# Transposing half of an activation by DMA, moving V's turn to a task of its own, opening a gate one step earlier, and putting PV before projections at the end in a statically scheduled attention kernel

## The chip, the cores and the metric

The kernel runs on one core of a Trainium2 chip. The metric is the device time of one execution in microseconds (us). The profiled execution of each kernel shows a span (first to last instruction) which is 1.7 to 3.5 us shorter than the device time of the same execution. All executions compared here are fast: none is more than 1.5% above the fastest of its kernel. TensorE does matrix products, VectorE and GpSimd elementwise work, ScalarE the exponentials; SyncE (SP) issues all DMAs.

## The reference

Two attention blocks over 2048 tokens, width 1024, 32 heads of 32, concatenated. A is plain softmax attention. B works on four segments of 512 tokens: causal softmax attention inside the segment, plus a read of a memory that earlier segments have written.

```
a:  q,k,v = x @ wqkv ;  o = softmax(q k^T / sqrt(32)) v ;  out = o @ wo
b:  for s in range(4):                      # segments of 512
        a_dot = softmax(q_s k_s^T / sqrt(32) + causal mask) v_s
        a_mem = (phi(q_s) @ M) / (phi(q_s) @ z + 1e-6)
        o_s   = sigmoid(beta) * a_mem + (1 - sigmoid(beta)) * a_dot
        M += phi(k_s)^T v_s ;  z += sum(phi(k_s))
    out = o @ wo
```

## The kernel before

The kernel is written by a scheduler. At build time it plays the program with a table of estimated costs, keeps a list of tasks (generators that yield what they wait for), and appends instructions to each engine's program in the order in which they would start. On the chip that order is fixed; only semaphore waits adapt. So a changed cost number or a changed condition moves the order of everything after it.

Scores of A come in 64 units (group g of four heads, 256 queries c), those of B in 32. A unit of A is 16 exponentials of 128x1024. `pick` takes the next unit from A or B. TensorE writes scores, ScalarE takes the exponential, TensorE multiplies by V ("PV") and sums the rows, VectorE normalises (`finish`), and projections (`out_proj`) follow.

```
def loads(self):                                  # A's x: 16 tiles of 128 rows
    for k in range(16):
        tile_in(k)                                # plain DMA
        if k == 1: self.load_WA(0, 0)             # weights of the keys
        if k == 3: self.load_WA(1, 0)             # queries
        if k == 5: self.load_WA(2, 0)             # V

def turn_A(self):                                 # each tile turned by 8 TensorE transposes
    for k in range(16):
        ...
        yield ("pe", self.ready(keys))
        def f(e): ... e.transpose(self.psb[:, bank, ...], src[...], self.ident[:, :])
        ...                                       # then one copy out by VectorE (two by ScalarE)

def a_prep(self, g):                              # keys, queries, V of one group
    for c in range(4):                            # chunks of 512 tokens
        yield ("ev", ("xA", c))                   # (g == 0)
        yield from proj(0, c)                     # keys
        self.events.add(("kA", g, c))
        if early:                                 # first group only
            if c == 0:
                ...
                yield from proj(1, 0)             # queries of chunk 0
                self.events.add(("sA", g, 0))
            yield from proj_V(c)                  # V in line, turned by a small DMA transpose

def pick(self):
    ...
    if b and b.kn >= 8 and ("amem", b.kn) not in self.events:
        b = None                                  # B barred until its memory read is done
    if a and b:
        it = b if b.kn < a.kn * SLOPE + LEAD else a

# b_prep(n), from segment 1 on: the memory read
    ...  den = Zb^T PH + 1e-6                     # one matmul, one VectorE op
    for q in range(4): reciprocal(den[:, cs])     # four VectorE ops
    ...  amem = (Mb^T PH) * gA * den
    self.events.add(("amem", n))

# schedule(): what TensorE does next when no scores are due
    full = len(self.ring_busy) > HIGH
    first = self.run if STICK and self.run else ("pv" if full else "side")
```

`self.run` is what TensorE did last, so the last line keeps it at projections ("side") or at PV. "Chunk" below is 512 keys of the first unit of A: four exponentials.

## Time and profile before

The median of the first three runs is 1203.21 us (1202.05 to 1205.38). The span of the profiled run is 1198.7 us. First the page's busy times by engine (PE is TensorE's matmul, PEld its weight load, DVE VectorE, ACT ScalarE).

```profile
span 1198.7 us, 37080 instructions
PE 1042.5 (87%) x16699; PEld 481.9 (40%) x16927; DVE 803.4 (67%) x1363; ACT 1125.4 (94%) x1256; POOL 116.5 (10%) x192
```

ScalarE is the limit. Its 1216 exponentials cannot be removed, so a schedule can win only its idle time. The view of busy time by stretch, for four stretches that I chose (the last begins when the last exponential ends):

```profile
core 0: us, PE busy (x) PEld busy (x) DVE busy (x) ACT busy (x) POOL busy (x), PEclk, DMA share, GB/s
0.00:16.00 16.00, 12.48 (x94) 6.92 (x96) 8.14 (x14) 3.55 (x5) 4.06 (x16) 1.00 0.94 293
16.00:54.00 38.00, 34.06 (x389) 15.48 (x394) 14.83 (x24) 23.97 (x29) 0.00 (x0) 1.00 0.25 56
54.00:1168.30 1114.30, 976.22 (x16114) 450.73 (x16323) 769.49 (x1307) 1097.89 (x1224) 112.39 (x176) 0.97 0.23 52
1168.30:1198.70 30.40, 19.70 (x117) 8.74 (x117) 10.99 (x20) 0.00 (x0) 0.00 (x0) 0.87 0.15 55
```

In each line the count of instructions is in brackets; PEclk is the share of its full clock that TensorE was granted, DMA share the mean busy share of the 16 DMA engines. Length less ScalarE's busy time is its idle: 12.4, 14.0, 16.4 and 30.4 us. I call these stretches first loads, start, middle and end. All idle numbers below are worked out like this.

The start, in the timeline of ScalarE (start, duration, operation, count, and in brackets the idle time before and what ended it):

```profile
15.99 3.77 ACT L532 ACTIVATE PT<-ps 128x1024 bf16<-128x1024 f32 x4 [6.09 <-PE ps L506]
23.68 0.77 ACT L467 ACTIVATE gcol<-ps 32x8 f32<-32x8 f32 x4 [3.92 <-PE ps L462]
26.70 3.83 ACT L532 ACTIVATE PT<-ps 128x1024 bf16<-128x1024 f32 x4 [2.25 <-PE ps L506]
33.49 3.77 ACT L532 ACTIVATE PT<-ps 128x1024 bf16<-128x1024 f32 x4 [2.97 <-PE ps L506]
39.80 9.27 ACT L532 ACTIVATE PT<-ps 128x1024 bf16<-128x1024 f32 x10 [2.53 <-PE ps L506]
51.34 18.44 ACT L532 ACTIVATE PT<-ps 128x1024 bf16<-128x1024 f32 x20 [2.27 <-PE ps L506]
```

The first four exponentials of each chunk start at 16.0, 26.7, 33.5 and 39.8, with waits for scores between.

The end, in the timeline of all engines (L674 with xA,OTA is A's output projection, L591 to L612 the normalisation of the last unit):

```profile
1163.39 4.84 ACT L532 ACTIVATE PT<-ps 128x1024 bf16<-128x1024 f32 x5
1166.10 12.03 PE L674 MATMUL ps<-xA,OTA 128*128 128x512 bf16 x54 [0.16 <-issue]
1179.05 0.28 PE L581 MATMUL ps<-PT,ones 128*32 128x256 bf16 x4
1179.39 0.69 DVE L591 COPY OL<-ps 128x512 f32<-128x512 f32 x1 [0.53 <-PE ps L581]
1182.56 0.42 DVE L612 TENSOR_TENSOR OTA<-OL,SQ 128x256 bf16<-128x256 f32 x1
1183.04 1.14 PE L674 MATMUL ps<-xA,OTA 128*128 128x512 bf16 x4 [3.70 <-DVE OTA L612]
```

TensorE still owes projection matmuls of earlier units when the exponentials end: a block of 54 starts at 1166.1, 2 us before that. The last PV comes after them, and then TensorE waits 3.7 us for the normalisation.

The view by tile, from 1000 us on, shows the scores of B (first line: tile KQB) and B's own output projection (second line: tile WoB). Duration min/median/max in ns, then first and last start:

```profile
L506 PE MATMUL ps<-KQB x72: 214/309/416, 1000.8 to 1061.2; 32*128 32x256 bf16 x48, 32*128 32x128 bf16 x24
L674 PE MATMUL ps<-WoB,OTB x58: 379/379/390, 1075.6 to 1102.8; 128*128 128x512 bf16 x58
```

### The profile page before, as it was taken

What the parts mean: (1) busy time and instruction counts of PE and PEld (TensorE: products, weight loads), DVE (VectorE), ACT (ScalarE), POOL (GpSimd) and SP (SyncE); (2) the same over time, 40 slices, a digit from 0 to 9 for tenths busy, and PEclk for the clock granted to TensorE, in tenths of its full rate; (3) what the DMA queues carried; (4) which work ended last, traced back from release to release, by engine and by line L of the source; (5) the groups of instructions that cost most, each with busy time, mean ns of one, the idle gap of its engine ahead of it and who ended that gap; (6) DMA issues with size and microseconds to landing.
All of it is one profiled execution on the core that took longest, in us unless ns stands there. A gap on an engine that the chain in (4) does not pass through costs nothing.

```text
span 1198.7 us, 37080 instructions
## 1 busy us (share of the span) xinstructions
PE 1042.5 (87%) x16699; PEld 481.9 (40%) x16927; DVE 803.4 (67%) x1363; ACT 1125.4 (94%) x1256; POOL 116.5 (10%) x192
## 2 busy tenths in 40 slices
PE   8998889999888888888988897978989887789996
PEld 4343444444344333334444443434444343334442
DVE  5248567576786687866777768677777668774443
ACT  3799999999999999999999999999999999999990
POOL 1001001010101020200111102010110102010000
PEclk9999999999999979899999998989999898989998
DMA  5461132243111122141212121211221110401101
GB/s 172 100 162 38 32 86 59 60 89 76 42 37 41 39 48 54 31 82 32 68 38 45 46 50 37 60 24 37 49 66 41 32 42 15 102 20 37 37 37 56
DMA packets 198344, 66.45 MB, mean 55 GB/s; under 512 B 189986, under 2 KB 189986, under 8 KB 198178
## 3 DMA queue, kind: packets, MB, share of 16 engines
q1 hardware_dynamic: 198178, 63.99, 23.1%
q8 instruction: 135, 2.21, 0.8%
q14 instruction: 31, 0.25, 0.1%
HBM read 39.85 MB, written 8.39 MB: 40 GB/s over the span
## 4 chain that ended last, share of the span: by engine, by line
ACT 47%; PE 40%; DVE 10%; issue 3%; DMA 1%; SPq 0%; DVEq 0%
ACT PT L532 46%; PE ps L674 21%; PE ps L581 9%; PE ps L506 8%; DVE SQ L604 2%; DVE OL L591 2%; DVE den L870 1%; ACT E L844 1%; DVE OL L608 1%; DVE amem L877 1%; DMA OTA<-in_A_x_dram 1%; DVE OTA L612 0%; DVE den L864 0%; DVE outsb L919 0%; DMA out_dram<-outsb 0%
## 5 line engine op out<-in xcount | busy, mean ns | idle before, releaser
L532 ACT ACTIVATE PT<-ps 128x1024 bf16<-128x1024 f32 (+1 forms) x1216 | 1102.4, 1039 | 32.4 <-PE ps L506 30.1
L581 PE MATMUL ps<-PT,ones 128*32 128x256 bf16 (+1 forms) x4864 | 295.6, 275 | 0.0
L581 PE MATMUL ps<-PT,VA 128*32 128x256 bf16 x4096 | 251.8, 277 | 20.9 <-ACT PT L532 15.0
L506 PE MATMUL ps<-QA,KA 32*128 32x256 bf16 x4096 | 213.2, 277 | 39.6 <-ACT PT L532 31.3
L604 DVE RECIPROCAL SQ<-OL 128x128 f32<-128x128 f32 x256 | 242.8, 948 | 4.9
L674 PE MATMUL ps<-xB,WB 128*128 128x512 bf16 x684 | 179.2, 383 | 21.2 <-issue 11.6
L674 PE MATMUL ps<-xA,WA 128*128 128x512 bf16 x695 | 181.6, 387 | 16.5 <-issue 8.7
L506 PEld LDWEIGHTS ps<-QA,KA 32*128 32x128 bf16 x4096 | 62.7, 92 | 224.8 <-ACT PT L532 201.0
L581 PEld LDWEIGHTS ps<-PT,VA 128*32 128x32 bf16 x4096 | 108.2, 95 | 111.3 <-issue 65.3
L552 POOL TENSOR_SCALAR_AFFINE_SELECT PT<-PT 128x512 bf16<-128x512 bf16 x128 | 85.9, 672 | 666.3 <-ACT PT L532 661.2
L581 PEld LDWEIGHTS ps<-PT,ones 128*32 128x32 bf16 x4864 | 131.6, 98 | 2.5
L591 DVE COPY OL<-ps 128x512 f32<-128x512 f32 x128 | 85.6, 669 | 30.3 <-PE ps L581 29.4
L674 PEld LDWEIGHTS ps<-xA,WA 128*128 128x128 bf16 x768 | 63.2, 99 | 93.9 <-issue 27.9
L674 PEld LDWEIGHTS ps<-xB,WB 128*128 128x128 bf16 x768 | 61.8, 98 | 95.2 <-issue 45.3
L919 DVE CAST outsb<-ps 128x512 bf16<-128x512 f32 x64 | 43.5, 680 | 76.2 <-PE ps L674 71.4
L870 DVE RECIPROCAL den<-den 128x128 f32<-128x128 f32 x96 | 91.2, 950 | 2.3
L684 DVE CAST KQB<-ps 128x512 bf16<-128x512 f32 x64 | 43.7, 683 | 57.8 <-PE ps L674 57.4
L674 PE MATMUL ps<-xA,OTA 128*128 128x512 bf16 x236 | 59.5, 391 | 8.5 <-DVE OTA L612 3.7
L674 PE MATMUL ps<-WoB,OTB 128*128 128x512 bf16 x232 | 59.7, 380 | 6.6 <-issue 2.9
L581 PE MATMUL ps<-PT,VB 128*32 128x256 bf16 (+1 forms) x768 | 50.8, 282 | 15.3 <-DVE OL L591 12.0
L608 DVE SCALAR_TENSOR_TENSOR OL<-OL,SQ 128x256 f32<-128x256 f32 x128 | 58.2, 455 | 2.7
L684 DVE CAST VT<-ps 128x512 bf16<-128x512 f32 x32 | 22.0, 687 | 47.7 <-PE ps L674 44.3
(64 smaller groups left out, 490.9 us busy)
## 6 DMA issues: line engine op xcount, KB each, us to landing
WB<-in_B_wk_dram SPq DMA_DIRECT2D x32, 256.0 KB, 3.0
WB<-in_B_wq_dram SPq DMA_DIRECT2D x32, 256.0 KB, 2.9
WB<-in_B_wv_dram SPq DMA_DIRECT2D x32, 256.0 KB, 3.2
out_dram<-outsb SPq DMA_DIRECT2D x32, 256.0 KB, 2.0
WA<-in_A_wqkv_dram SPq DMA_DIRECT2D x24, 256.0 KB, 3.8
OTA<-in_A_x_dram SPq DMA_DIRECT2D x16, 256.0 KB, 5.6
WoB<-in_B_wo_dram SPq DMA_DIRECT2D x1, 2048.0 KB, 10.2
xA<-in_A_wo_dram SPq DMA_DIRECT2D x1, 2048.0 KB, 10.3
```

Source lines behind the costliest of these rows:

```text
L506: ins = e.matmul(o, l, r, start=True, stop=True)
L532: op = R.op("ACT", lambda e: e.activation(self.PT[:, s0:s0 + n, 0:width], self.ps[:, banks[0]:banks[0] + n, 0:width], ACTF.Exp, bias=cb, s ...
L552: mo = R.op("POOL", lambda e, ap=ap, pat=pat: e.affine_select(ap, ap, pattern=pat, compare_op=ALU.is_ge, fill=0.0, base=0, channel_multipl ...
L581: ins = e.matmul(o, l, r, start=start, stop=end, skip_group_check=True)
L591: R.op("DVE", lambda e: e.tensor_copy(self.OL[x][:, :], self.ps[:, OLB, :]), r=[("ps", OLB)], w=[("OL", x)], cost=0.66)
L604: R.op("DVE", lambda e, cs=cs: e.reciprocal(rec[:, cs], L[:, cs]), r=[ko], w=[k], cost=0.93)
L608: R.op("DVE", lambda e: e.scalar_tensor_tensor(L, L, 1.0, rec, ALU.mult, ALU.add, accum_out=self.rng[:, u.seq:u.seq + 1]), r=[k, ko], w=[k ...
L674: ins = e.matmul(o, l, rh, start=a, stop=z)
L684: op = self.R.op("DVE", lambda e: e.tensor_copy(dst, self.ps[:, bank, :]), r=[("ps", bank)], w=[dkey], cost=0.66)
L844: ex = R.op("ACT", lambda e: e.activation(self.E[:, k0:k1, :], KQ[:, k0:k1, :], ACTF.Exp), r=[("KQB", b, k) for k in range(k0, k1)], w=["E ...
L870: R.op("DVE", lambda e, cs=cs: e.reciprocal(self.den[:, cs], self.den[:, cs]), r=["den"], w=["den"], cost=0.9)
L919: op = R.op("DVE", lambda e, ns=ns, bank=bank, ob=ob: e.tensor_copy(self.outsb[ob][:, ns], self.ps[:, bank, :]), r=[("ps", bank)], w=[("ou ...
```

## The change

Its intent: the first keys need not wait for 16 tiles to be turned on TensorE, V of the first group need not sit between two key projections, and B's scores need not wait for the memory read. Five parts can be told apart: (1) chunks 2 and 3 of A's x are loaded by one DMA transpose each, only eight tiles are turned on TensorE; (2) the first V runs in a task of its own, one chunk behind the keys, turned by TensorE; two PSUM banks (buffers into which TensorE writes) lent to these tasks go back earlier; (3) B's scores are gated on the sum in the denominator ("den") and the finish of the unit waits for the memory read instead; (4) when the banks of the scores have been given up at the end, PV goes before projections; (5) the planning numbers for the load of B's x.

```
+TURNS = 2
+GATE = "den"
@@ load_xB                                                    # (5)
-                   ..., issue=5.0, mb=1.0)
+                   ..., issue=1.0, mb=2.0)
@@ loads, turn_A                                              # (1)
-        for k in range(16):
+        for k in range(4 * TURNS):
             tile_in(k)
...
-            if k == 5:
+            if k == 4 * TURNS - 1:
                 self.load_WA(2, 0)
+        for c in range(TURNS, 4):
+            R.dma(lambda e, c=c: e.dma_start(self.xA[:, :, 512*c:512*c+512],
+                  self.A_x[0][512*c:512*c+512, :], transpose=True), ..., issue=1.0, mb=2.0)
+            self.events.add(("xA", c))
@@ a_prep                                                     # (2)
+            if early:
+                ...                            # 4 TensorE transposes, one VectorE copy
+            else:
+                self.turn_V(vt[:, :], key, dst, ("VA", b, c))
+        def values():
+            yield ("ev", ("WA", 2, g))
+            for c in range(4):
+                yield ("ev", ("kA", g, min(c + 1, 3)))
+                yield from proj_V(c)
+            self.load_WA(2, g + 1)
...
-                    yield ("ev", ("WA", 2, g))
-                yield from proj_V(c)
+                    self.spawn(values(), (-1, 1.5), "valuesA0")
@@ schedule                                                   # (2)
-            if self.lent and ("vA", 0, 3) in ev:
+            if self.lent and ("vA", 0, 2) in ev:
...
-                if not self.bank_busy & set(self.lent) and nslot == 0:
+                if not self.bank_busy & set(self.lent):
@@ finish, b_prep, pick                                       # (3)
             else:
+                yield ("ev", ("amem", u.kn))
...
+            self.events.add(("den", n))        # right after the sum, before the reciprocals
...
-        if b and b.kn >= 8 and ("amem", b.kn) not in self.events:
+        if b and b.kn >= 8 and (GATE, b.kn) not in self.events:
@@ schedule                                                   # (4)
-            full = len(self.ring_busy) > HIGH
-            first = self.run if STICK and self.run else ("pv" if full else "side")
+            full = len(self.ring_busy) > HIGH or not self.slots
+            first = self.run if STICK and self.run and self.slots else ("pv" if full else "side")
```

More of the change, by code (lines that the diff above doesn't have):

```diff
@@ L368, in load_xB @@
         self.R.dma(lambda e: e.dma_start(self.xB[b][:, :, :], src, transpose=True),
-                   w=[("xB", b, i) for i in range(NI)], issue=5.0, mb=1.0)
+                   w=[("xB", b, i) for i in range(NI)], issue=1.0, mb=2.0)
         self.events.add(("xB", s))
@@ L387, in loads @@
                 self.load_WA(1, 0)
-            if k == 5:
+            if k == 4 * TURNS - 1:
                 self.load_WA(2, 0)
+        for c in range(TURNS, 4):
+            R.dma(lambda e, c=c: e.dma_start(self.xA[:, :, 512 * c:512 * c + 512], self.A_x[0][512 * c:512 * c + 512, :], transpose=True),
+                  w=[("xA", i, c) for i in range(NI)], issue=1.0, mb=2.0)
+            self.events.add(("xA", c))
         R.dma(lambda e: e.dma_start(self.beta[0:1, :], self.B_beta.rearrange("(a n) -> a n", a=1)), w=["beta"], issue=0.5, mb=0.01)
@@ L405, in turn_A @@
         R = self.R
-        for k in range(16):
+        for k in range(4 * TURNS):
             src, keys = self.stage(k)
@@ L728, in a_prep @@
         k_ = 0
+        early = g == 0 and not self.shifted
         def pace():
@@ L745, in proj_V, with f @@
             yield from self.proj_T(self.WA[2], ("WA", 2), lambda i: self.xA[:, i, cs], lambda i: ("xA", i, c), vt[:, :], key)
-            self.turn_V(vt[:, :], key, self.VA[b][:, 4 * c:4 * c + 4, :], ("VA", b, c))
-            self.events.add(("vA", g, c))
+            dst = self.VA[b][:, 4 * c:4 * c + 4, :]
+            if early:
+                bank = yield ("bank",)
+                yield ("pe", self.ready([key]))
+                def f(e, bank=bank):
+                    for t in range(4):
+                        ins = e.transpose(self.psb[:, bank, P * t:P * t + P], vt[:, P * t:P * t + P], self.ident[:, :])
+                    return ins
+                R.op("PE", f, r=[key, "ident"], w=[("ps", bank)], cost=0.3)
+                op = R.op("DVE", lambda e, bank=bank: e.tensor_copy(dst, self.psb[:, bank, 0:512].rearrange("p (t n) -> p t n", t=4)),
+                          r=[("ps", bank)], w=[("VA", b, c)], cost=0.36)
+                self.bank_release(bank, op)
+            else:
+                self.turn_V(vt[:, :], key, dst, ("VA", b, c))
+            self.events.add(("vA", g, c))
+        def values():
[4 more added lines that the diff above has]
+            self.load_WA(2, g + 1)
         def total(k):
@@ L753, in total @@
                  r=[("cbt", b, 0), ("cbt", b, 1 + k)], w=[("cbA", b, k)], cost=0.1)
-        early = g == 0 and not self.shifted
         yield ("ev", ("WA", 0, g))
@@ L774, in a_prep @@
         yield from self.a_norm(g, 0, range(4), cb[:, 4:5], ("cbt", b, 0))
+        if early:
+            yield ("ev", ("vA", g, 3))
         for c in range(1 if early else 0, 4):
@@ L789, in a_prep @@
             self.load_WA(1, g + 1)
-            self.load_WA(2, g + 1)
+            if not early:
+                self.load_WA(2, g + 1)
         else:
```

## The prediction

> **What bounds it now.** ScalarE: busy 1125.4 of 1198.7 us (94%), 1102.4 of it the 1216 exponentials of 1.04 us. The change removes none, so it can only win from 73 us of idle. The view of busy time by stretch places them: 0-16 us, 12.4 idle; 16-54 us, 14.0 idle; 54-1168 us, 16.4 idle in 1114; 1168-1199 us, 30.4 idle. TensorE is busy 87%.
>
> **16-54 us.** ScalarE's timeline shows bursts of four exponentials (3.8 us), one per chunk of keys, starting at 16.0, 26.7, 33.5 and 39.8, with waits for scores between, and 2.3 us more before 51.3. TensorE fills them: transposing the other 11-12 tiles of x until 21.8, then keys and V of a chunk one after the other (1.7-1.9 us each, plus 1.4 us until the scores start).
>
> **Removed and added.** Half of 128 TensorE transposes goes (8 tiles, each about 0.6 us on TensorE and a 0.69 us copy on VectorE: 5 us of each). Added: two DMA transposes of 1 MB. B's x has the same shape: 4.4-5.7 us to issue, 7.7-8.4 to land (about 130 GB/s; the Trainium skill, "DMA: Bandwidth & Descriptors", Latency and other measured facts, gives 261 GB/s for one kernel; this trace is slower and I use the trace). Issued after eight tile loads, near 7.5 and 12.5 us, they should land near 16-17 and 21-23. Four DMA turns of V (2.4 us to landing) become 16 TensorE transposes and four copies, about 0.3 + 0.4-0.7 us each.
>
> **On the critical path.** Keys of chunk 1 need no longer wait for 12 tiles and V: their exponentials can follow the first burst (about 20 instead of 26.7). Chunk 2 follows near 24-25. Chunk 3 is ordered late by the static schedule: near 30-32, not 39.8. I expect 8-10 us saved here, and 1-2 of the wait before 51.3, as the lent banks return earlier. The first key projection waits in TensorE's order for the fifth tile, landed at 9.75; with one weight load later, up to 0.5 us.
>
> **Tail.** After the last exponential (1168.2) TensorE runs 54 projection matmuls, 12 us, before the last PV (1178.1-1179.3), then idles 3.7 us for the normalisation. The change prefers PV once the score banks are given up. That normalisation then hides under the projections: about 3.5 us saved.
>
> **B's gate.** Scores of B may start when the denominator is summed, about four reciprocals (3.8 us) and a matmul earlier. While B is barred A's scores run instead, so ScalarE is fed: all its waits for scores after 200 us are 12.1 us, in 19 pieces, many where the granted clock is 0.86-0.93. I expect 0-3 us. Reordering may shift the middle by +-4 us.
>
> **Sum.** -9 -1.5 -0.3 -3.5 -1 = about -15: 1188 us. Two per cent would need 24 us.
>
> **Signs.** If right, the second, third and fourth bursts start near 20, 25 and 31; ScalarE's idle in 16-54 falls from 14 to 3-5; 54-1168 keeps about 1102 us busy with 13-17 idle; the last PV comes directly after the last exponential and the 3.7 us wait is gone.
>
> **What would make it wrong.** The two transposes block SP's queue for some 10 us or land past 25 us (chunk 3 then near 36 or later, gain 4 less); they slow the last tile loads; V, now a task with higher priority, pushes the keys back; finishing B units, which now waits for the memory read, holds back PV and fills the ring; TensorE is throttled longer.

## The result, and the profile after

The changed kernel takes 1187.83 us (median of 4, 1186.62 to 1190.14); the kernel before, over the runs taken by then, 1202.63 us (median of 4). The ratio is 0.988, with a 95% interval of 0.985 to 0.991. A ratio here is the mean time of one kernel's fast runs over that of the other's of the same rounds, so not quite the ratio of the medians.

The total lies on the predicted 1188. The parts do not. The page and the view by stretch, after:

```profile
span 1184.9 us, 36949 instructions
PE 1028.6 (87%) x16650; PEld 480.5 (41%) x16880; DVE 796.3 (67%) x1359; ACT 1124.7 (95%) x1256; POOL 116.3 (10%) x192
```

```profile
0.00:16.00 16.00, 12.71 (x100) 7.24 (x101) 8.75 (x15) 3.54 (x4) 4.08 (x16) 1.00 0.98 253
16.00:54.00 38.00, 34.80 (x467) 15.48 (x470) 12.62 (x23) 31.34 (x37) 0.00 (x0) 1.00 0.58 107
54.00:1164.90 1110.90, 970.64 (x16040) 453.43 (x16254) 767.06 (x1306) 1089.80 (x1216) 112.18 (x176) 0.97 0.22 51
1164.90:1184.90 20.00, 10.45 (x61) 4.34 (x59) 7.92 (x15) 0.04 (x1) 0.00 (x0) 0.88 0.12 44
```

| idle of ScalarE, us | first loads | start | middle | end |
|---|---|---|---|---|
| before | 12.4 | 14.0 | 16.4 | 30.4 |
| predicted change | -0.3 | -9 to -11 | about -1 | -3.5 |
| after | 12.5 | 6.7 | 21.1 | 20.0 |
| measured change | 0 | -7.3 | +4.7 | -10.4 |

The start gained less than predicted, the end three times as much, and the middle gave 4.7 us of these 17.7 back. The timeline of ScalarE at the start, after:

```profile
16.23 7.49 ACT L538 ACTIVATE PT<-ps 128x1024 bf16<-128x1024 f32 x8 [6.53 <-PE ps L512]
25.48 1.94 ACT L538 ACTIVATE PT<-ps 128x1024 bf16<-128x1024 f32 x2 [1.76 <-PE ps L512]
28.42 1.94 ACT L538 ACTIVATE PT<-ps 128x1024 bf16<-128x1024 f32 x2 [1.00 <-PE ps L512]
32.22 2.85 ACT L538 ACTIVATE PT<-ps 128x1024 bf16<-128x1024 f32 x3 [1.86 <-PE ps L512]
34.95 0.76 ACT L473 ACTIVATE gcol<-ps 32x8 f32<-32x8 f32 x4
40.39 18.52 ACT L538 ACTIVATE PT<-ps 128x1024 bf16<-128x1024 f32 x20 [1.65 <-PE ps L512]
```

The first two chunks are now one run of eight exponentials; chunks 3 and 4 start at 25.5 and 32.2. The two DMA transposes, in the view by line (start, and the time from issue to landing):

```profile
L393 SPq DMA_TRANSPOSE xA<-in_A_x_dram x2: 4801/5698/6596, 7.3 to 14.0; - x2
DMA to landing us min/median/max: 6.9/8.5/10.1
```

The bursts come nearly where they were predicted (20, 25, 31), but the second half of chunk 3's keys waits once more, and so does the stretch before 40.4. TensorE is busy 34.8 of these 38 us, no less than before (34.1): the time it saved on turning went to scores, V and PV that now come earlier.

The end, after:

```profile
1159.31 5.63 ACT L538 ACTIVATE PT<-ps 128x1024 bf16<-128x1024 f32 x6 [0.88 <-PE ps L512]
1163.87 1.90 PE L681 MATMUL ps<-xA,OTA 128*128 128x512 bf16 x7
1166.03 0.28 PE L587 MATMUL ps<-PT,ones 128*32 128x256 bf16 x4
1166.25 1.90 PE L681 MATMUL ps<-xA,OTA 128*128 128x512 bf16 x8
1170.23 0.42 DVE L618 TENSOR_TENSOR OTA<-OL,SQ 128x256 bf16<-128x256 f32 x1
1170.72 7.08 PE L681 MATMUL ps<-xA,OTA 128*128 128x512 bf16 x31 [2.57 <-DVE OTA L618]
```

The block of 54 owed matmuls is gone: eight remain beside the last 32 (31 of them in the trace, which can lack a few matmul records), and 2.6 us of the wait for the normalisation are still there, because too little is left to fill it. B's scores and B's projection, from 1000 us on:

```profile
L512 PE MATMUL ps<-KQB x40: 214/272/278, 1001.3 to 1025.0; 32*128 32x256 bf16 x24, 32*128 32x128 bf16 x16
L681 PE MATMUL ps<-WoB,OTB x58: 379/379/390, 1034.0 to 1060.6; 128*128 128x512 bf16 x58
```

B's last scores come 36 us earlier, and B's projection (64 matmuls, 58 of them in either trace) is finished 42 us earlier, at about 1061. From then until 1165 the only projections left are A's, and TensorE catches up: after the last exponential it runs 44 of A's projection matmuls, where it ran 76 before.

### The profile page after: what moved, and what is told of

Its sections match the earlier page's. It is cut to its first block, busy times and chain, and to the rows that moved or that the text cites. A ratio compares the mean times of both kernels' runs of the same rounds, so it can differ in the third digit from the quotient of the medians.

```text
span 1184.9 us, 36949 instructions
## 1 busy us (share of the span) xinstructions
PE 1028.6 (87%) x16650; PEld 480.5 (41%) x16880; DVE 796.3 (67%) x1359; ACT 1124.7 (95%) x1256; POOL 116.3 (10%) x192
## 4 chain that ended last, share of the span: by engine, by line
ACT 48%; PE 39%; DVE 9%; issue 2%; DMA 0%; SPq 0%; DVEq 0%
ACT PT L538 47%; PE ps L681 22%; PE ps L587 9%; PE ps L512 8%; DVE SQ L610 3%; DVE OL L597 1%; ACT E L874 1%; DVE OL L614 1%; DVE OTA L618 0%; DMA OTA<-in_A_x_dram 0%; DVE amem L908 0%; DVE KQB L691 0%; DVE KA L691 0%; DVE OL L638 0%; DVE OTB L640 0%
## 5 line engine op out<-in xcount | busy, mean ns | idle before, releaser
L587 PE MATMUL ps<-PT,ones 128*32 128x256 bf16 x4864 | 294.3, 275 | 0.0
L512 PE MATMUL ps<-QA,KA 32*128 32x256 bf16 x4096 | 210.3, 279 | 48.2 <-ACT PT L538 41.1
L681 PE MATMUL ps<-xB,WB 128*128 128x512 bf16 x689 | 176.6, 380 | 25.1 <-issue 10.9
L597 DVE COPY OL<-ps 128x512 f32<-128x512 f32 x128 | 85.7, 669 | 23.0 <-PE ps L587 21.6
L587 PE MATMUL ps<-PT,VB 128*32 128x256 bf16 (+1 forms) x768 | 47.9, 270 | 13.8 <-DVE OL L597 9.8
L691 DVE CAST QA<-ps 128x512 bf16<-128x512 f32 x32 | 22.1, 691 | 42.5 <-PE ps L681 42.2
```

Of the source, the lines that this page charges most:

```text
L512: ins = e.matmul(o, l, r, start=True, stop=True)
L587: ins = e.matmul(o, l, r, start=start, stop=end, skip_group_check=True)
L597: R.op("DVE", lambda e: e.tensor_copy(self.OL[x][:, :], self.ps[:, OLB, :]), r=[("ps", OLB)], w=[("OL", x)], cost=0.66)
L681: ins = e.matmul(o, l, rh, start=a, stop=z)
L691: op = self.R.op("DVE", lambda e: e.tensor_copy(dst, self.ps[:, bank, :]), r=[("ps", bank)], w=[dkey], cost=0.66)
```

## The experiments

Twelve kernels were run, all correct. My theory after reading the two traces: the gate pulls B forward and so unloads the end; the start gains by its own parts; the rule of the end has little left to do. The first rival: the earlier start pulled B forward. Idle in the table at the end of this section is from the profiled run of each; times are medians.

**only_gate: the kernel before with part (3) alone.** Edit: the three hunks marked (3).

> The kernel before with the new gate of B alone. Theory (gate): B's units run earlier, the last B scores fall from 1061 us to about 1030, B's output projection ends near 1065, so no projections are left over and the stretch after the last exponential shrinks from 30.5 us to about 20-23; some 2-5 us are given back as idle of ScalarE in the middle. Time about 1196, ratio 0.993-0.997. Rival (start): the gate does nothing, the earlier start pulled B forward; last B scores stay near 1060, stretch after the last exponential near 30, ratio 0.998-1.002.

Measured: 1199.43 us, ratio 0.998 (0.996 to 0.999). The view by stretch from the last exponential on, and the tiles KQB and WoB from 900 us on:

```profile
1176.05:1198.70 22.65, 12.22 (x61) 4.98 (x60) 8.02 (x15) 0.00 (x1) 0.00 (x0) 0.82 0.11 39
L506 PE MATMUL ps<-KQB x120: 214/278/416, 922.7 to 1038.2; 32*128 32x256 bf16 x80, 32*128 32x128 bf16 x40
L675 PE MATMUL ps<-WoB,OTB x73: 379/379/390, 902.6 to 1081.8; 128*128 128x512 bf16 x73
```

The gate alone takes 7.8 us from the end (30.4 to 22.6), as expected, with the last B score at 1038. But the middle rose by 8.6 us, from 16.4 to 25.0, where I had expected 2 to 5; that gave it back, and the time moved less than expected.

**only_tail: the kernel before with part (4) alone.**

> The kernel before with the new rule of the end alone (PV first once the score banks are given up). As predicted: last PV directly after the last exponential, the 3.7 us wait of TensorE gone, ratio 0.997 (about 3.5 us); everything up to about 1160 us the same instruction order as before. Rival: the order of the last 54 projection matmuls and PV changes nothing since VectorE's copies queue: ratio 0.999-1.001.

Measured: 1195.97 us, ratio 0.995 (0.993 to 0.997). The instruction order differs from the kernel before only at one small place and at the very end; ScalarE's order is the same. The timeline after the last exponential:

```profile
1172.65 17.44 PE L674 MATMUL ps<-xA,OTA 128*128 128x512 bf16 x78
1179.11 0.42 DVE L612 TENSOR_TENSOR OTA<-OL,SQ 128x256 bf16<-128x256 f32 x1
```

PV came first, then all projections in one piece, with the normalisation hidden under them. The end is 25.0 us instead of 30.4: the predicted mechanism, 5.4 instead of 3.5 us. The middle of this profile is 19.2, with the same order as the 16.4 of before: 3 us in the middle is what one profile can differ from another for no reason of the schedule. (The profiled run is the slowest of the six, whose spans go from 1191.0 to 1196.9.)

**only_start: the changed kernel with the old gate and the old rule of the end.** Edit: `GATE = "amem"`, and the two lines of (4) as before.

> The changed kernel with the old gate and the old rule of the end: loads, turning, V's task and lent banks alone. Theory (gate): ScalarE's idle in 16-54 us near 6.7 as in the changed kernel, stretch after the last exponential still near 30, last B scores near 1050; time about 1195, ratio 0.993-0.995. Rival (start): last B scores near 1025, stretch at the end near 20, ratio 0.987-0.990.

Measured: 1199.75 us, ratio 0.999 (0.997 to 1.001). The start keeps its gain (6.7 us idle, as in the changed kernel), the end stays at 29.0 us, the last B score comes at 1059.0:

```profile
1165.40:1194.40 29.00, 18.26 (x117) 8.40 (x117) 11.09 (x20) 0.00 (x1) 0.00 (x0) 0.96 0.15 57
```

So the rival is out: behind the old gate the early start does not pull B forward. (With the gate open it does, from 1038 in only_gate to 1025 in no_tail.) The time is nearly 5 us worse than my own expectation: the middle is 20.1, and in all five runs the device time is 3.2 to 4.0 us above the span, where the kernel before has 2.0 to 3.4 and the changed kernel 1.7 to 1.8. I have no cause for that difference. The granted clock of these runs is low too, which the section after the experiments takes up.

**no_tail: the changed kernel without part (4).**

> The changed kernel without the new rule of the end. Theory (gate): as no projections are left over, the rule has little to reorder: within 2 us of the changed kernel, ratio to before 0.988-0.990. Rival (the predicted 3.5 us of this rule are part of the gain): 3-4 us slower than the changed kernel, ratio 0.991-0.992.

Measured: 1189.56 us, ratio 0.990 (0.988 to 0.992), end 20.8 us:

```profile
1165.16:1186.00 20.84, 10.30 (x60) 4.46 (x59) 8.02 (x15) 0.00 (x0) 0.00 (x0) 0.94 0.12 42
```

Against the changed kernel the rule is worth 0.8 us of the end once the gate has unloaded it; alone it was worth 5.4. The two parts draw on the same idle time. This kernel is also start plus gate: 12 us faster than before, while each alone gave 2 to 3 (for the start alone the interval includes no gain at all).

**no_dmaT: all 16 tiles turned on TensorE again, the rest of the change kept.** Edit: `TURNS = 4`, and V's weights loaded at `k == 5`.

> The changed kernel with all 16 tiles of A's x turned on TensorE (the weights of V loaded after tile 5, as before); V's task, the gate and the rule of the end stay. Theory: the saving in 16-54 us comes mainly from the keys of chunk 1 not waiting behind 12 tiles, so ScalarE's idle in 16-54 rises from 6.7 to 11-13 us, second burst near 25; time about 1193, ratio 0.991-0.994. Rival (V's own task gives the saving, the DMA transposes nothing): idle stays below 8, ratio 0.987-0.990.

Measured: 1196.32 us, ratio 0.997 (0.995 to 1.000). ScalarE's timeline:

```profile
15.56 3.77 ACT L538 ACTIVATE PT<-ps 128x1024 bf16<-128x1024 f32 x4 [5.93 <-PE ps L512]
24.32 1.94 ACT L538 ACTIVATE PT<-ps 128x1024 bf16<-128x1024 f32 x2 [4.99 <-PE ps L468]
```

The second burst is back at 24.3 and the start idles 13.1 us, almost the 14.0 of before. The DMA transposes are necessary for the gain of the start; V's task without them does next to nothing.

**old_V: V in line and turned by small DMA transposes, the rest kept.** Edit: `yield from proj_V(c)` back in the loop, `values` not spawned, `turn_V` used.

> The changed kernel with the first V as before: computed in line between the keys and turned by four small DMA transposes of the same queue as the big ones. Theory: the small transposes queue behind the two 1 MB ones (issued until 18.8 us) and land after 22 us, keys of chunk 1 wait for V of chunk 0 only by 1.9 us of TensorE: idle in 16-54 near 9-11. Rival (V's task is as important as the DMA transposes): idle 12-14. Time 1190-1195.

Measured: 1196.92 us, ratio 0.998 (0.995 to 1.000). The start idles 10.1 us, as expected. V's task is worth 3.4 us of the start on top of the DMA transposes; the DMA transposes with V in line give 3.9 (14.0 to 10.1). Within V's task, its order and its turn on TensorE were changed together, and the earlier return of the two banks was never undone alone; what each is worth is not shown. In this run and in no_dmaT the times are 8 to 9 us worse than the changed kernel's, and worse than I expected. The start explains 3.4 and 6.4 us of it; the middle and the end, longer by 1.1 to 1.6 us each, and in old_V 1.6 us more of ScalarE's busy time make up the difference of the spans (1192.7 and 1194.1 against 1184.9). I don't assign those small terms to a cause.

**late_B: the changed kernel with B's pace lowered.** Edit: `SLOPE = 0.54` for `0.65`. The gate stays open, but B is made late.

> The changed kernel with the pace of B lowered (slope 0.54 for 0.65), so that B ends late although the gate is open. Theory (what shortens the end is that B's last units come early): last B scores at 1055-1075 us, B's projections end after 1095, projections of A are left over and the stretch after the last exponential grows from 20.0 to 24-26; time 1190-1195. Rival (the gate itself or the order of PV shortens the end): stretch stays at 20-21 whatever the time of the last B scores.

Measured: 1200.10 us, ratio 0.999 (0.997 to 1.001). The end and B's scores:

```profile
1173.30:1199.60 26.30, 19.27 (x101) 8.57 (x101) 11.19 (x20) 0.01 (x1) 0.00 (x0) 0.91 0.17 63
L512 PE MATMUL ps<-KQB x144: 214/272/278, 909.4 to 1079.7; 32*128 32x256 bf16 x96, 32*128 32x128 bf16 x48
```

With B's last score at 1080 TensorE again owes projections (101 matmul records in the end instead of 61), and the end is 26.3 us although gate and rule are those of the changed kernel. So the end follows the time at which B is done, and not the gate as such. This knob reorders much else, so alone it would be weak evidence, but the table below agrees: with the old rule of the end, 1061, 1059, 1038 and 1025 go with 30.4, 29.0, 22.6 and 20.8 us; with the new rule, 1080 and 1065 with 26.3 and 25.0, and everything up to 1033 with 19.9 to 21.9. Half of the 12 us lost is here; the rest is in the start (8.4) and in the middle (27.3).

**free_gate: B not gated at all.** Edit: `GATE = "sB"`, an event that is always there when B is considered.

> The changed kernel with B's scores not gated at all (they need their keys and queries only). Theory: B ends earlier still (last B scores at 990-1015 us), but as no projections are left over already the stretch after the last exponential stays at 20; middle idle 20-26; within 4 us of the changed kernel, ratio to before 0.985-0.992. Rival (each step of the gate is worth as much as the last): ratio below 0.983.

Measured: 1243.39 us, ratio 1.035 (1.033 to 1.037). B was done earliest of all (last score at 971), and the end stayed at 21.8, near the expected 20. But between 400 and 800 us ScalarE idled 50 us. I had not foreseen it. The waits of ScalarE from 380 to 820 us (total, times, longest):

```profile
ACT PT L538 <- PE ps L512: 49.9, 32, 8.7
```

A reading that fits the code: a unit of B that is scored early reaches `finish` before its memory read, holds its output buffer there, and the last step of PV of the unit after the next may not be issued; the exponentials have nowhere to go, so no scores are written. The next kernel tests that reading.

**split_free: no gate, but the finish does not hold its buffer.** Edit:

```
-                yield ("ev", ("amem", u.kn))
...
-                stt(O, O, gB, rec)            # into the same buffer
-                tensor_tensor(dst, O, am, ADD)
+                stt(dst, O, gB, rec)          # out at once
+                self.events.add(("fin", u.seq))
+                yield ("ev", ("amem", u.kn))
+                tensor_tensor(dst, dst, am, ADD)
```

> B's scores not gated at all, as in the run of 1243 us, but a finished unit of B is written out normalised first and the memory read is added to it later, so its buffer, and with it PV, no longer waits for the memory read. Theory (the run without a gate lost 50 us because finished units waited for the memory read and held back PV): ScalarE's idle in 400-800 us falls from 50 to 10-15, last B scores before 1000 us, stretch at the end 20-22; time 1185-1195. Rival (the scores of B in a row, or B's preparation, cost the 50 us): idle in 400-800 stays above 30, time above 1215.

Measured: 1198.57 us, ratio 0.997 (0.995 to 0.999). The same view of waits:

```profile
ACT PT L538 <- PE ps L512: 14.8, 13, 3.0
```

Idle of ScalarE in 400 to 800 fell from 50.5 to 13.0 us, as the reading said it would, and the rival's 30 or more did not come. The time missed my range by 4 us, with 29.5 us idle in the middle as a whole. No gate is worse than a gate even without the held buffer; why the middle stays that long is open.

**split_den: the same split, with the gate on the denominator.**

> The changed kernel with the same late adding of the memory read, gate on the denominator kept. Theory: the denominator comes early enough that finished units seldom wait, so little changes: within 3 us of the changed kernel, 1184-1191, ratio 0.986-0.991. Rival (the 4.8 us more of idle in the middle are units that wait for the memory read): middle idle falls from 21 to 16, time 1182-1184.

Measured: 1188.93 us, ratio 0.989 (0.987 to 0.991); start, middle and end within 0.4 us of the changed kernel. With this gate, units do not lose time to a waiting finish. So that is not what lengthened the middle by 4.7 us.

**old_xbcost: part (5) undone.** Edit: `issue=5.0, mb=1.0` for the load of B's x. It changes no work, only the plan.

> The changed kernel with the old planning numbers for the load of B's x (they only steer the order of the static schedule, the work is the same). It is the last part of the change and at once a gauge of how far another order of the same work moves the time. Theory: start and end as in the changed kernel (6-8 and 20-22 us idle), middle idle anywhere in 16-26; time 1184-1194. Rival (this number is a real part of the gain): 1196 or more with a longer stretch at the end.

Measured: 1188.05 us, ratio 0.987 (0.985 to 0.990). Another order of the same work (last B score at 1011, middle 19.1, end 21.9), the same time.

**turn1: one step further, three chunks by DMA.** Edit: `TURNS = 1`, and `mb=1.4` for the transposes.

> The changed kernel carried one step further: three quarters of A's x transposed by DMA, only four tiles turned on TensorE, and the schedule told that such a transpose takes 5.6 instead of 8 us (6.9 and 10.1 to landing were measured). Theory (TensorE is what holds the start back): four tiles fewer take 2.5 us of TensorE and of VectorE out of the first 16-54 us, idle there 3-6 instead of 6.7; if the middle keeps 17-25, time 1183-1189. Rival (the DMA of chunk 1 lands too late, past 15 us, and the copies of the first tiles share bandwidth with it): first burst later than 16.2 or second burst later than 21, idle in 0-54 above 19.2, time 1188-1193.

Measured: 1188.31 us, ratio 0.988 (0.985 to 0.990). First loads and start together idle 19.3 us, as in the changed kernel (19.1): the first burst came at 14.9 instead of 16.2, but the start idled 1.2 us longer. My theory of 3 to 6 us in the start is refuted (7.9), and so is its premise: in the changed kernel all 64 transposes on TensorE run between 3.6 and 13.1 us, so four tiles fewer take nothing off TensorE in 16 to 54 us (35.0 us busy there, 34.8 in the changed kernel). The rival's late burst did not come either.

| kernel | time, us | start | middle | end | last B score |
|---|---|---|---|---|---|
| before | 1202.63 | 14.0 | 16.4 | 30.4 | 1061 |
| changed | 1187.83 | 6.7 | 21.1 | 20.0 | 1025 |
| only_gate | 1199.43 | 14.0 | 25.0 | 22.6 | 1038 |
| only_tail | 1195.97 | 14.4 | 19.2 | 25.0 | 1065 |
| only_start | 1199.75 | 6.7 | 20.1 | 29.0 | 1059 |
| no_tail | 1189.56 | 6.7 | 21.3 | 20.8 | 1025 |
| no_dmaT | 1196.32 | 13.1 | 22.6 | 21.2 | 1033 |
| old_V | 1196.92 | 10.1 | 22.2 | 21.6 | 1031 |
| late_B | 1200.10 | 8.4 | 27.3 | 26.3 | 1080 |
| free_gate | 1243.39 | 6.8 | 69.7 | 21.8 | 971 |
| split_free | 1198.57 | 6.9 | 29.5 | 21.5 | 976 |
| split_den | 1188.93 | 6.7 | 21.5 | 20.0 | 1026 |
| old_xbcost | 1188.05 | 7.1 | 19.1 | 21.9 | 1011 |
| turn1 | 1188.31 | 7.9 | 21.4 | 19.9 | 1026 |

No version beats the changed kernel clearly.

## Why the prediction was right, and where it was not

**The total** (1188 predicted, 1187.83 measured) was right, and so was its frame: ScalarE's busy time did not change (1125.4 and 1124.7 us), and only its idle time could be won. But three terms of the sum were mis-sized and happened to cancel, so that the total came out to within a microsecond is luck. Between the two profiled runs (1201.71 and 1186.67 us) 13.0 of the 15.0 us are idle of ScalarE, 0.7 its busy time, and 1.2 the part of the device time outside the span, which the prediction did not treat.

**Start: right mechanism, too large.** Predicted -9 -1.5 us, measured -7.3. The DMA transposes landed about where predicted: issued at 7.3 and 14.0, landed at 17.4 and 20.9 (10.1 and 6.9 us). no_dmaT and old_V show that both halves are needed. What I left out is that TensorE has to do keys, V, its turns, queries and PV in the same 38 us and was busy for 34.8 of them, so the chunks could not follow each other without gaps. This fits the profile but is not tested: turn1 was meant to, and took nothing off TensorE in this stretch.

**Tail: right mechanism, the wrong share of the gain.** "The change prefers PV once the score banks are given up ... about 3.5 us saved". Alone this rule gave 5.4 us (only_tail); within the change it gave 0.8, since there were no owed projections left to hide the normalisation under. Accordingly the sign "the 3.7 us wait is gone" failed: 2.6 us of it remain.

**Gate: the step that failed.** "While B is barred A's scores run instead, so ScalarE is fed ... I expect 0-3 us." I looked only at waits of ScalarE around the gate, and those are indeed small. I did not ask what the delay does to the time at which B is done. Opening the gate moved B's last score 23 us (only_gate) and, with the start, 34 us (only_start to no_tail) forward, and B's projections with it; the end fell by 7.8 and 8.2 us. late_B made B late with another knob and got a long end back. In time, the gate gave 3 us alone, inside the "0-3 us", but by luck: 7.8 us won at the end and 8.6 lost in the middle, neither of them foreseen. On top of the start it gave about 10 us (ratio 0.999 to 0.990). That does not make it the largest part: the start on top of the gate gave 9 (0.998 to 0.990), and the rule of the end was the best of the three alone (6 us).

**Middle: inside the stated +-4 us only nearly.** It grew by 4.7 us. split_den rules out that finished units of B wait. I cannot assign it. Two things bound it: the same order of ScalarE's work gave 16.4 in one profile and 19.2 in another, and each of the twelve other orders tried gave 19.1 or more. So the old order may be a slightly favourable one in the middle, and a reordering pays for its gain there; with one profile each and a scatter of 3 us that is only argued.

**Parts do not add.** Start alone gave 2 us, gate alone 3, both together 12. The start and end windows add well (7.3, and 7.8 to 8.2); the middle is where the sum breaks: 25.0 for the gate alone, 20.1 for the start alone, 21.3 for both. Some of the rest is in the unexplained difference of device time and span.

**A rival that no run excludes: the granted clock.** The record lists TensorE's mean granted clock for every run. Over the 32 runs of the kernel before that were made beside the experiments, the same program, the span goes from 1194.9 to 1202.8 us and the clock from 0.972 down to 0.963; a straight line through them falls 0.8 us for each 0.001 (correlation -0.95). The kernels differ in it too: on average 0.967 before, 0.971 changed, 0.964 in only_start, 0.973 in no_tail. If the same slope holds between kernels, which is an estimate and not shown, about 3 of the 13 us by which the spans fell go with the clock, and about 7 of the 8.5 us by which the spans of no_tail are below those of only_start. At one clock, start, gate and both together would then have won about 6, 2 and 7 us of span: the parts would nearly add, and the gate would give back in the middle most of what it wins at the end, as it does in the profile of only_gate. Whether the order of work sets the clock (the runs of only_start have 0.961 to 0.967, those of no_tail 0.972 to 0.975, in the same rounds), or something else sets both, is open. The end does not hang on this: there TensorE has 117 matmul records to run in only_start and 60 in no_tail.

## What to carry to other kernels

When a gate or a priority delays one of two interleaved streams, don't price it only by the bottleneck engine's waits at that place: look at when the delayed stream ends and what its last work then collides with after the bottleneck engine has finished. Open such a gate as far as the buffers behind it allow and no further: here one step took 8 us off the end, and the next cost 55 us. And in a static schedule, read a change by stretches of the bottleneck's idle time, since a total that comes out as predicted can hide terms that cancel. Before you assign what is left, compare the granted clock of the runs.

## What the Trainium skill lacked or had wrong

- "DMA: Bandwidth & Descriptors", Latency and other measured facts, gives 261 GB/s for a DMA transpose in one kernel. While nothing but the second transpose was moving in the changed kernel (17.3 to 20.4 us), its DMA view shows 288 to 291 GB/s, somewhat more than the page's figure. What the page does not give is the time from issue to landing: 1 MB (512x1024 bf16 from HBM) took 6.9 to 10.1 us, which is only 104 to 152 GB/s (1.05 MB over the time), and 2 MB back to back took from 7.3 to 20.9 us, 154 GB/s. The 130 GB/s of the prediction are of this second kind, and not to be compared with 261.
- The same page gives no time for which a transpose of this size holds the issuing queue (its cycle counts are for small tiles and for SBUF to SBUF). Here it was 4.2 to 7.2 us for each 1 MB of A's x over all runs that do it, during which SyncE issued nothing else (the load of beta moved from 12.4 to 18.8 us).
- "TensorE: Matmul & The Clock Gate", Part 4: PE-mode transpose, gives about 275 ns for a 128x128 transpose in a kernel. Here the median was 219 ns, and eight pipelined ones took 0.62 us together, so a tile's cost is nearer 78 ns per transpose.
- No page that I read says how dips of the granted clock show in an engine other than TensorE, or in the time of a whole kernel. Here the span of one kernel fell 0.8 us for each 0.001 of mean clock over 32 runs. In windows of 20 us between 60 and 1160 us, the 9 of 55 with a clock below 0.97 held 9.3 of the 16.3 us of ScalarE's idle before, and 10 of 55 held 11.6 of 20.9 after. That the lower clock causes the idle is not shown.
- No page explains why the device time exceeds the span by 1.7 to 1.8 us in every run of some kernels and by 3.2 to 4.0 in every run of another with almost the same code.
